# Score tiles of the first batch kept in eight slots of one large buffer, its late store cut in two, and the second batch's scores and the first values moved to later steps

## The chip, the cores and the metric

One NeuronCore of a Trainium2 chip runs one program. The metric is device time in microseconds (us), the median of several executions. The parts of the core that matter here: TensorE (PE in the profile), VectorE (DVE), ScalarE (ACT), GpSimd (POOL), and SyncE (SP), whose queue issues every DMA of this kernel. Each of them runs its own list of instructions in order and waits on semaphores for the others.

## What is computed

Attention with a mixing of the heads before and after the softmax, and then a gated expert without a nonlinearity, over 8 batches (B), 12 heads (H), 448 positions (S) and head width 64 (D):

```
scores = scale * q @ k^T                              # per batch and head, 448 x 448
scores = einsum('bhij,hg->bgij', scores, w_pre)       # heads mixed
attn   = softmax over j
attn   = einsum('bhij,hg->bgij', attn, w_post)        # heads mixed again
x      = attn @ v                                     # to (8*448) x 768
out    = ((x @ w1) * (x @ w2)) @ w3 @ w_out
```

The weights of the expert come as 64-bit floats and are turned into pairs of 32-bit parts on the chip.

## The kernel before, in words

**Scores through DRAM.** The mixing of heads needs all 12 heads of one row i on the partitions, while q @ k^T yields one head at a time. So `qk` (L166) makes the scores of one group (b, p, c): batch b, pair of heads p, and 128 rows of i (c = 0 to 2; a group with c = 3 takes the last 64 rows of two pairs). Four matmuls write two PSUM banks, 0 and 1 for the first group of a step and 6 and 7 for a second one; ACT copies the two banks to an SBUF tile `st` of 128 x 2 x 448 floats (L179, L180); and SP stores the tile in `raw_d[b]` in DRAM at the start of the next step (448 KB; a group with c = 3 takes two stores of 224 KB). `fetch` (L195) reads `raw_d` back as tiles `r` with (i, head) on the partitions, four steps ahead of their use; two `r` buffers stand ready.

**Steps.** The main loop (L889) runs over steps n of 10 rows of i, 45 steps per batch. A fetch, mix, exponential and second mix handle two steps at once, so work comes in pairs of steps: in an even step the maxima (`largest`, DVE L227) and `exp` (ACT L235); in an odd step `scale`, `post` (PE L260, into the two banks `pso`) and the next `mix` (PE L220). `put` (ACT L274) copies `pso` into a tile `mt`, which gathers 150 columns of i for attn @ v. `av` (PE L301) multiplies `mt` with the values and writes PSUM bank 0; its first run stands in step 19, its second in step 21.

**Weights beside it.** In the first 49 steps (up to `SWITCH`) the fold w3 @ w_out fills PE's free time (`folding`, PE L360, 384 matmuls); the function `shares` gives steps 18 and later a number of fold matmuls by how much else each step has, among it the score groups. Its operands are converted from words: SP loads `cs`, ACT and DVE convert (L110, L121 to L124, L129), POOL subtracts (L130), two pieces in a pair of steps.

**The buffers that the change touches.** The first six score groups (0, p, 0) are made ahead of the loop and lie together in one large tile `sz`, the first of the two buffers of the tag `mt` (L774): 5376 of its 7200 columns. Their first 48 rows are stored at once (FIRST, L31), the other 80 rows in one late store of 1680 KB (L805, issued by `held()` in L881). Each later `st` tile comes from a pool with two buffers: `qp` for odd pairs p of batch 0, `kp` for even ones and for all other batches (L178). The first `mt` tile takes the second `mt` buffer; the second one, `mt[0, 1]`, takes the buffer of `sz`, and its first copy comes at the end of step 17.

**What sets the order.** The dictionary `qks` (L809 to L819) says which groups stand at the end of which step: one group of batch 0 in each of steps 0 to 14, then batch 1 at steps int(11 + i * 28/21), i = 0 to 20, so steps 11, 12, 13, 15, 16, 17, 19 and on to 37; each c = 0 group has its keys and queries loaded six steps earlier (`load_kq`, 448 KB). The six loads of the first batch's values (`load_v`, 256 KB each) stand in steps 6 to 11 (L930). SP uses eight DMA semaphores in turn, so each DMA waits until the one eight places before it has landed.

Of the kernel before, what the change touches and what calls it, by code (L numbers as in the profile page):

```python
# [6 lines left out]
F32 = mybir.dt.float32  # L7
# [8 lines left out]
B, H, S, D = 8, 12, 448, 64  # L16
DM, FF = 768, 1024
HP = H // 2
IB = 10
GI = H * IB  # L20
NB = -(-S // IB)
QT, NJ = 128, 4
# [5 lines left out]
PP = 64  # L28
JB = S // PP
SETS = NB * B // 2  # L30
FIRST = 48  # L31
# [4 lines left out]
N_UP, NS = 20, 50  # L36
DEEP = 5
ONE = 2
# [12 lines left out]
class Kernel:  # L51
# [108 lines left out]
    def parts(self, b, p, c):  # L160
# [3 lines left out]
        return [(self.kqs[b, p], j * PP, S) for p, j in pairs]  # L164

    def qk(self, b, p, c, banks):  # L166


        nc = self.nc
# [5 lines left out]
        if b == c == 0:  # L175
            st = self.sz[:, 2 * p:2 * p + 2]
        else:
            st = (self.qp if b == 0 and p % 2 else self.kp).tile([128, 2, S], F32, tag="st", name=f"st{b}_{p}_{c}", bufs=2)  # L178
        nc.scalar.copy(st[:, 0], ps[0])  # L179
# [7 lines left out]
        n = QT if b or c else FIRST  # L187
# [553 lines left out]
    def run(self):  # L741
        nc, tc = self.nc, self.tc
# [31 lines left out]
        self.sz = self.mp.tile([QT, NJ, H, GB * IB], F32, tag="mt", name="sz")  # L774
        self.sz = self.sz.rearrange("p j g i -> p (j g i)")[:, :H * S].rearrange("p (h j) -> p h j", h=H)
        w = self.kp.tile([128, 2, S], F32, tag="st", name="wpre_s", bufs=2)[:, 0, :PP]
# [4 lines left out]
        for p in self.pso:  # L781
            for s in range(2):
                at = (2 * NJ - 2 + s) * HK
# [11 lines left out]
        held = []  # L795
# [7 lines left out]
        for f in held:  # L803
            f()
        held = lambda: nc.sync.dma_start(self.raw_d[0][FIRST:QT], self.sz[FIRST:])  # L805

# [5 lines left out]
        for b in range(1, B):  # L812
            first, per = (11, 28 / 21) if b == 1 else ((b - 1) * NB - 6, NB / 21)
            units = [(b, p, c) for g in range(0, HP, 2) for p, c in [*itertools.product((g, g + 1), range(3)), (g + 1, 3)]]
            for i, (b, p, c) in enumerate(units):
                n = int(first + i * per) | (b > 1)
                qks.setdefault(n, []).append((b, p, c))
                if c == 0:
                    loads.setdefault(max(n - 6, 0), []).append((b, p))  # L819
# [57 lines left out]
        for m in range(LF // 2):  # L877
            self.fetch(m)
        next(fold_pieces)
        next(fold_pieces)  # L880
        held()  # L881
        next(fold_pieces)
# [6 lines left out]
        for n in range(N + 6):  # L889
# [38 lines left out]
            if n + 3 < HP:  # L928
                others(n + 3)
            elif HP <= n < 2 * HP:  # L930
                self.load_v()
# [120 lines left out]
```

## Time and profile before

| | |
|---|---|
| median of 3 executions | 1441.89 us (1441.69 to 1447.07) |
| the profiled execution | 1437.83 us |
| its span, first to last instruction | 1436.1 us |
| mean granted TensorE clock | 0.986 |
| busy share of the span: PE, ACT, DVE, POOL | 96%, 58%, 52%, 43% |
| DMA over the span | 416.87 MB, mean 290 GB/s |

Times of single instructions are counted from the start of the span. A row of the timeline gives the start, the length and the instruction, and in brackets how long the engine had been idle before it and what ended that. A row of the waits gives the waiting engine and line, what it waited for, the sum in us, the number of times and the longest. A row of the windows gives each engine's busy time in a stretch, the granted clock (1.00 is full speed), the busy share of the DMA engines and what they moved.

### The profile page before, as it was taken

Reading aid. Unit: us, or ns where it says so; the run is one execution under the profiler, and the core shown is the slowest. Engines: PE = TensorE matmul, PEld = TensorE weight load, DVE = VectorE, ACT = ScalarE, POOL = GpSimd, SP = SyncE. Lnnn points to the kernel's source line nnn. Section 1 sums busy time; section 2 is a strip of 40 time slices with the busy share of each in tenths; the row PEclk is TensorE's granted clock in tenths of the full one; section 3 lists DMA queues with packets and bytes.
Section 4 is the critical chain, followed back from the end, with each engine's and each line's share of the span. In section 5 each row is a group of like instructions: output and inputs, shape, how many; then the busy total and the mean of one; then the engine's idle time right before and its main releaser. Section 6 shows DMA issues by size and latency. Waiting matters only on the chain.

```text
span 1436.1 us, 45775 instructions
## 1 busy us (share of the span) xinstructions
PE 1382.4 (96%) x18684; PEld 1055.2 (73%) x18684; DVE 741.1 (52%) x1497; ACT 832.4 (58%) x1952; POOL 620.3 (43%) x754
## 2 busy tenths in 40 slices
PE   5889999999999999999999999999999999999998
PEld 2457786776677667776777777777777777899988
DVE  6867566767544544432444436334444446345563
ACT  4867666777766666665656556556555445422231
POOL 2433233434433544532345336334335446446693
PEclk7989999999999999999999999999999999999999
DMA  8998789999999999999989979799879757698775
GB/s 294 366 326 279 236 270 322 320 312 317 324 286 348 355 356 330 362 346 349 287 275 290 320 259 280 249 323 354 288 229 281 241 177 223 195 337 270 231 232 171
DMA packets 203761, 416.87 MB, mean 290 GB/s; under 512 B 20528, under 2 KB 120112, under 8 KB 203472
## 3 DMA queue, kind: packets, MB, share of 16 engines
q1 hardware_dynamic: 203552, 413.94, 87.6%
q8 instruction: 149, 2.44, 0.7%
q14 instruction: 60, 0.49, 0.1%
HBM read 279.77 MB, written 134.09 MB: 288 GB/s over the span
## 4 chain that ended last, share of the span: by engine, by line
PE 82%; DMA 8%; DVE 4%; ACT 2%; issue 1%; POOL 1%; SPq 0%; DVEq 0%; POOLq 0%; ACTq 0%
PE e L702 21%; PE psa L301 11%; PE pso L260 10%; PE psm L220 9%; PE psq L174 7%; PE eg L522 5%; PE psf L360 4%; PE eo L553 4%; PE e2o L702 4%; PE e1o L702 4%; PE e3o L702 4%; DMA wu<-w_d 3%; DMA r<-raw_d 2%; DMA raw_d<-st 2%; ACT e L235 1%
## 5 line engine op out<-in xcount | busy, mean ns | idle before, releaser
L247 POOL TENSOR_SCALAR w<-wpo,ri 128x60 f32<-128x60 f32 x360 | 180.7, 518 | 485.1 <-DVE ri L245 465.3
L227 DVE TENSOR_REDUCE mn<-psm 128x1 f32<-128x448 f32 x360 | 207.7, 618 | 321.6 <-PE psm L220 321.3
L274 ACT COPY mt<-pso 128x480 f32<-128x480 f32 x352 | 197.9, 621 | 185.8 <-PE pso L260 185.6
L702 PE MATMUL e<-eh,wu 128*128 128x448 f32 x1008 | 296.8, 371 | 6.4 <-DVE c L656 3.2
L235 ACT ACTIVATE e<-psm,mn 128x448 f32<-128x448 f32 x360 | 226.8, 643 | 7.9 <-DVE mn L227 7.9
L702 PEld LDWEIGHTS e<-eh,wu 128*128 128x128 f32 x1008 | 187.5, 188 | 52.2 <-issue 26.8
L260 PEld LDWEIGHTS pso<-w,e 60*64 60x64 f32 x10080 | 175.2, 135 | 51.0 <-issue 42.5
L220 PE MATMUL psm<-r,wsc 60*64 60x448 f32 (+1 forms) x1440 | 191.2, 550 | 19.1 <-DVE cx L124 8.3
L260 PE MATMUL pso<-w,e 60*64 60x60 f32 x10080 | 199.1, 224 | 0.4 <-ACT mt L274 0.3
L702 PE MATMUL e<-el,wu 128*128 128x448 f32 x504 | 186.9, 371 | 0.0
L301 PE MATMUL psa<-mt,v 128*64 128x150 f32 (+1 forms) x2304 | 156.9, 292 | 4.1 <-ACT st L179 4.1
L301 PEld LDWEIGHTS psa<-mt,v 128*64 128x64 f32 x2304 | 143.6, 137 | 20.1 <-ACT st L179 6.7
L174 PE MATMUL psq<-kq 64*64 64x448 f32 x1176 | 154.6, 542 | 2.4 <-ACT st L179 2.4
L656 DVE TENSOR_TENSOR c<-c,e 128x448 f32<-128x448 f32 x168 | 101.7, 618 | 87.7 <-PE e L702 82.9
L179 ACT COPY st<-psq 128x448 f32<-128x448 f32 x162 | 86.4, 533 | 73.7 <-ACT mt L274 34.1
L522 PE MATMUL eg<-xh,wu 128*128 128x448 f32 x384 | 119.2, 381 | 6.3 <-DMA wu<-w_d 6.3
L641 POOL TENSOR_TENSOR el<-x,eh 128x448 fp32r<-128x448 f32 x90 | 103.7, 1170 | 32.8 <-ACT eh L640 29.9
L702 PEld LDWEIGHTS e<-el,wu 128*128 128x128 f32 x504 | 94.6, 188 | 22.5 <-issue 14.1
L174 PEld LDWEIGHTS psq<-kq 64*64 64x64 f32 x1176 | 60.8, 135 | 56.4 <-issue 28.8
L522 PEld LDWEIGHTS eg<-xh,wu 128*128 128x128 f32 x384 | 71.9, 190 | 38.7 <-issue 24.0
L244 DVE TENSOR_SCALAR sa<-sm 128x2 f32<-128x2 f32 x180 | 34.9, 194 | 113.6 <-ACT e L235 113.1
L180 ACT COPY st<-psq 128x448 f32<-128x448 f32 x162 | 87.6, 541 | 0.0
(99 smaller groups left out, 2010.1 us busy)
## 6 DMA issues: line engine op xcount, KB each, us to landing
r<-raw_d SPq DMA_DIRECT2D x344, 210.0 KB, 5.1
raw_d<-st SPq DMA_DIRECT2D x138, 448.0 KB, 6.1
wu<-w_d SPq DMA_DIRECT2D x104, 384.0 KB, 6.7
wu<-s_d SPq DMA_DIRECT2D x96, 384.0 KB, 4.8
wu<-w_d SPq DMA_DIRECT2D x51, 512.0 KB, 5.5
kq<-kq SPq DMA_DIRECT2D x42, 448.0 KB, 7.0
wu<-s_d SPq DMA_DIRECT2D x36, 512.0 KB, 4.9
x<-x_d SPq DMA_DIRECT2D x72, 224.0 KB, 5.7
```

Source lines behind the costliest of these rows:

```text
L174: nc.tensor.matmul(ps[s][z * PP:(z + 1) * PP], t[rows, q:q + PP], t[rows, k:k + S], start=True, stop=True)
L220: nc.tensor.matmul(ps[s][c * PP:(c + 1) * PP, :S], self.wsc[k], r[k, c], start=True, stop=True)
L227: self.nc.vector.tensor_reduce(mn[:, s:s + 1], self.psm[m][s][:, :S], axis=AX.X, op=ALU.min)
L235: nc.scalar.activation(e, p[:, :S], AF.Exp, bias=mn[:, s:s + 1], scale=-1.0, accum_out=sm[:, s:s + 1])
L247: nc.gpsimd.tensor_scalar_mul(w2[:, s], self.wpo, ri[:, s:s + 1])
L260: nc.tensor.matmul(self.pso[c][z * PP:(z + 1) * PP, at:at + HK], e[k, j * PP:(j + 1) * PP], w2s[k, s], start=True, stop=True)
L274: self.nc.scalar.copy(dst.rearrange("p j g (s i) -> p j s g i", s=2), src)
L301: nc.tensor.matmul(self.psa[rows, g % 3, :W], v[:, j, rows], mt[:, j, 2 * g + s, :W], start=(j == 0), stop=(j == NJ - 1))
L522: nc.tensor.matmul(p, u[:, k % (K1 // 2), x], xs[y][:, k], start=(k == 0 and t == 0), stop=(k == K1 - 1 and t == 2))
L641: nc.gpsimd.tensor_tensor(lo, x, hi.bitcast(F32), op=ALU.subtract)
L656: nc.vector.tensor_tensor(a[out], a[to[0]], p, op=ALU.add)
L702: nc.tensor.matmul(p, w[:, k, x], ops[m, k][y], start=(k == 0 and t == 0), stop=(k == nk - 1 and t == 2))
```

## The change

Four edits. (1) Score tiles made up to step 14 (RING) lie in eight slots of 896 columns of the `sz` buffer, taken in turn: the first two are the free columns behind the first scores, the next ones overwrite slots of the first scores. Later tiles all come from `kp`; `qp` has no `st` tiles any more. (2) The late store is cut into rows 48 to 63 (344 KB), issued ahead of the next load of words, and rows 64 to 127 (1376 KB), issued one place later. (3) Batch 1's groups stand at steps int(14 + 1.2 i): 14, 15, 16, 17, 18, 20 to 24, 26 to 30, 32 to 36 and 38; the loads of their keys move with them. (4) The loads of the first values stand in steps 11 to 16.

```diff
-DEEP = 5
+DEEP, RING = 5, 14
...
+    def next_st(self, name):
+        if self.step > RING:
+            return self.kp.tile([128, 2, S], F32, tag="st", name=name, bufs=2)
+        self.n_st += 1
+        at = (self.n_st + HP - 1) % 8 * 2 * S
+        return self.sz_all[:, at:at + 2 * S].rearrange("p (h j) -> p h j", h=2)
...
-            st = (self.qp if b == 0 and p % 2 else self.kp).tile([128, 2, S], F32, tag="st", name=f"st{b}_{p}_{c}", bufs=2)
+            st = self.next_st(f"st{b}_{p}_{c}")
...
-        self.sz = self.sz.rearrange("p j g i -> p (j g i)")[:, :H * S].rearrange("p (h j) -> p h j", h=H)
+        self.sz_all, self.n_st = self.sz.rearrange("p j g i -> p (j g i)"), 0
+        self.sz = self.sz_all[:, :H * S].rearrange("p (h j) -> p h j", h=H)
...
-        held = lambda: nc.sync.dma_start(self.raw_d[0][FIRST:QT], self.sz[FIRST:])
+        rest = [lambda k=k: nc.sync.dma_start(self.raw_d[0][k], self.sz[k]) for k in (slice(FIRST, PP), slice(PP, QT))]
...
-            first, per = (11, 28 / 21) if b == 1 else ((b - 1) * NB - 6, NB / 21)
+            first, per = (14, 1.2) if b == 1 else ((b - 1) * NB - 6, NB / 21)
...
+        rest[0]()
         next(fold_pieces)
         next(fold_pieces)
-        held()
+        rest[1]()
...
-            elif HP <= n < 2 * HP:
+            elif HP <= n - 5 < 2 * HP:
```

Where this moves instructions, first on SP's queue ahead of the loop. `r0` to `r2` are fetched score tiles, `cs3` to `cs5` words of weights, `kqz2` a piece of keys. Before:

```order
L202 DMA r1_222<-raw0_d_62 60x2x448 x2
L103 DMA cs3_225<-wo 128x768
L805 DMA raw0_d_62<-sz_136 80x5376
L103 DMA cs4_238<-wo 128x768
L103 DMA cs5_240<-wo 128x768
L873 DMA kqz2_128<-kq0 128x320
L202 DMA r2_258<-raw0_d_62 60x2x448 x2
L873 DMA kqz3_130<-kq0 128x320
```

And of the changed kernel, in the same place:

```order
L209 DMA r1_222<-raw0_d_62 60x2x448 x2
L813 DMA raw0_d_62<-sz_136 16x5376
L103 DMA cs3_226<-wo 128x768
L813 DMA raw0_d_62<-sz_136 64x5376
L103 DMA cs4_239<-wo 128x768
L103 DMA cs5_241<-wo 128x768
L881 DMA kqz2_128<-kq0 128x320
L209 DMA r2_259<-raw0_d_62 60x2x448 x2
L881 DMA kqz3_130<-kq0 128x320
```

The fetch `r2` needs rows 40 to 59, so of the late store it now waits for the first, smaller part alone; the second part still stands behind `cs3`.

The second place is ACT at the ends of steps 17 and 18 with the semaphores that each instruction waits for (DMAHW0 to DMAHW7 are those of SP's DMAs). `mt0_1` is the second `mt` tile, `st1_1_2` the tile of group (1, 1, 2). Before:

```order
L274 COPY mt0_0_414<-pso0_141 128x4x2x12x5 [waits PE_49]
L274 COPY mt0_1_1165<-pso1_142 128x4x2x12x5 [waits PE_49]
L179 COPY st1_1_2_1180<-psq1_1_2_0_1174 128x448 [waits DMAHW1_49,PE_49]
L180 COPY st1_1_2_1180<-psq1_1_2_1_1175 128x448 [waits PE_49]
L129 CAST fw1_1127<-cx20_1132 128x3x128 [waits DVE_49]
L110 ACTIVATE cm21_1196<-cs21_988 128x256 [waits DMAHW3_49,Activation_49]
L235 ACTIVATE e9_0_1214,sm9_1213<-psm9_0_1166,mn9_1191 128x448 [waits DVE_49]
```

And of the changed kernel:

```order
L281 COPY mt0_0_412<-pso0_141 128x4x2x12x5 [waits PE_49]
L281 COPY mt0_1_1130<-pso1_142 128x4x2x12x5 [waits DMAHW4_49,DMAHW3_49,DMAHW5_49,DMAHW2_49,DMAHW6_49,DMAHW1_49,DMAHW7_49,DMAHW0_49,PE_49]
L186 COPY st1_1_0_1145<-psq1_1_0_0_1139 128x448 [waits DMAHW6_49,PE_49]
L187 COPY st1_1_0_1145<-psq1_1_0_1_1140 128x448 [waits PE_49]
L129 CAST fw1_1092<-cx20_1097 128x3x128 [waits DVE_49]
L110 ACTIVATE cm21_1159<-cs21_939 128x256 [waits Activation_49]
L242 ACTIVATE e9_0_1176,sm9_1175<-psm9_0_1131,mn9_1154 128x448 [waits DVE_49]
L242 ACTIVATE e9_1_1178,sm9_1175<-psm9_1_1132,mn9_1154 128x448 [waits DVE_49]
L186 COPY st1_1_1_1194<-psq1_1_1_0_1188 128x448 [waits DMAHW2_49,PE_49]
```

The copy into `mt0_1` has got waits for DMAs, those of the stores out of the slots. Behind it two score tiles, of steps 17 and 18, each wait for a DMA: with `kp`'s two buffers these are the stores of the groups of steps 15 and 16, (1, 0, 1) and (1, 0, 2). Before, there was one such tile here, (1, 1, 2), which waits for the store of (1, 1, 0).

The third place is PE from the mix of step 17 to the first values matmuls in step 19. Before:

```order
L220 MATMUL psm9_1_1167<-r9_980,wsc_138 64x448
L174 MATMUL psq1_1_2_0_1174<-kq1_1_682 64x448
L174 MATMUL psq1_1_2_1_1175<-kq1_1_682 64x448
L174 MATMUL psq1_1_2_0_1174<-kq1_1_682 64x448
L174 MATMUL psq1_1_2_1_1175<-kq1_1_682 64x448
L360 MATMUL psf1_0_1203<-fo_148,fw0_227 128x384 x19
L301 MATMUL psa0_0_0_1235<-mt0_0_414,v0_0_540 64x150 x8
```

And of the changed kernel:

```order
L227 MATMUL psm9_1_1132<-r9_932,wsc_138 64x448
L181 MATMUL psq1_1_0_0_1139<-kq1_1_769 64x448
L181 MATMUL psq1_1_0_1_1140<-kq1_1_769 64x448
L181 MATMUL psq1_1_0_0_1139<-kq1_1_769 64x448
L181 MATMUL psq1_1_0_1_1140<-kq1_1_769 64x448
L367 MATMUL psf1_0_1166<-fo_148,fw0_228 128x384 x16
L181 MATMUL psq1_1_1_0_1188<-kq1_1_769 64x448
L181 MATMUL psq1_1_1_1_1189<-kq1_1_769 64x448
L181 MATMUL psq1_1_1_0_1188<-kq1_1_769 64x448
L181 MATMUL psq1_1_1_1_1189<-kq1_1_769 64x448
L308 MATMUL psa0_0_0_1205<-mt0_0_412,v0_0_767 64x150 x8
```

A score group now stands between step 18's folds and the first values matmul, and step 18 has 16 folds where it had 19. Counted from the start of the program, the groups of scores ahead of the first values matmul are 26 where they were 27, and the folds 40 where they were 43.

## The prediction

> **What bounds the kernel now.** I read the page first, then the windows, then who waited for whom in the first 100 us.
>
> ```profile
> span 1436.1 us, 45775 instructions
> PE 1382.4 (96%) x18684; PEld 1055.2 (73%) x18684; DVE 741.1 (52%) x1497; ACT 832.4 (58%) x1952; POOL 620.3 (43%) x754
> ```
>
> PE is busy for 96% of the span, so 54 us are idle. The windows show where the change works: busy us of each engine with its instructions, granted clock, DMA share, GB/s.
>
> ```profile
> core 0: us, PE busy (x) PEld busy (x) DVE busy (x) ACT busy (x) POOL busy (x), PEclk, DMA share, GB/s
> 31.00:58.00 27.00, 22.55 (x348) 11.11 (x348) 25.47 (x49) 23.96 (x58) 12.72 (x17) 0.94 1.02 360
> 58.00:72.00 14.00, 11.56 (x172) 6.13 (x166) 11.18 (x23) 9.26 (x23) 5.23 (x7) 0.87 1.03 374
> 72.00:85.00 13.00, 9.31 (x95) 4.75 (x88) 6.66 (x13) 9.28 (x22) 3.82 (x5) 0.50 1.04 377
> 85.00:96.00 11.00, 8.54 (x106) 5.39 (x99) 9.46 (x18) 6.49 (x16) 3.94 (x5) 0.99 1.01 351
> 111.00:220.00 109.00, 108.36 (x1504) 85.98 (x1500) 69.70 (x145) 71.98 (x174) 31.50 (x46) 1.00 0.84 266
> ```
>
> There are three stretches. Up to 58 us DVE is nearly full (25.47 of 27 us). From 58 to 96 us no engine is full, PE's clock sinks to half, and the DMA engines are busy throughout at 351 to 377 GB/s. From 111 us PE has hardly a gap (108.36 of 109), and DMA has room. After about 96 us, then, PE's work sets the end, and what counts is when PE gets there and how much work it has done by then.
>
> ACT's timeline shows the waits that the change aims at (start, length, instruction, idle before):
>
> ```profile
> 51.43 0.61 ACT L235 ACTIVATE e<-psm,mn 128x448 f32<-128x448 f32 x1
> 58.19 0.64 ACT L235 ACTIVATE e<-psm,mn 128x448 f32<-128x448 f32 x1
> 70.45 0.53 ACT L179 COPY st<-psq 128x448 f32<-128x448 f32 x1 [2.90 <-PE psm L220]
> 74.11 0.53 ACT L179 COPY st<-psq 128x448 f32<-128x448 f32 x1 [2.69 <-DMA raw_d<-st]
> 90.57 1.10 ACT L274 COPY mt<-pso 128x480 f32<-128x480 f32 x2
> 95.72 0.53 ACT L179 COPY st<-psq 128x448 f32<-128x448 f32 x1 [4.05 <-DMA raw_d<-st]
> 97.33 0.64 ACT L235 ACTIVATE e<-psm,mn 128x448 f32<-128x448 f32 x1
> ```
>
> The exponentials of steps 8 and 10 stand 6.76 us apart: that is the engines' own pace for a pair of steps. Step 18's comes at 97.33, although four such pairs would end at 58.19 + 4 * 6.76 = 85.2. The copies at 74.11 and 95.72 wait for a store to free their tile. The one at 70.45 names PE, but its matmuls were long done; its tile is that of step 9's group, whose store left late, so it is a DMA too. The last wait is the one that PE feels:
>
> ```profile
> 60.29 1.77 PE L220 MATMUL psm<-r,wsc 60*64 60x448 f32 x8
> 90.58 3.59 PE L360 MATMUL psf<-fo,fw 128*128 128x384 f32 x19
> 96.31 3.28 PE L301 MATMUL psa<-mt,v 128*64 128x150 f32 x48 [2.13 <-ACT st L179]
> 101.14 0.98 PE L174 MATMUL psq<-kq 64*64 64x448 f32 x8
> 106.47 3.28 PE L301 MATMUL psa<-mt,v 128*64 128x150 f32 x48 [0.64 <-ACT st L179]
> ```
>
> Step 19's first values matmul (96.31) writes bank 0, so it waits for the copy at 95.72, which waits for the store of group (1, 1, 0). I call this copy the gate.
>
> **Part by part: the slots.** They remove the waits for tiles in steps 11 to 14 (the 2.90 and 2.69 above, and shorter ones). But the gate moves, it does not go. The changed order has two tiles behind each other from `kp`, in steps 17 and 18; the second waits for the store of (1, 0, 2), and the values matmul waits for that copy. So I ask when that store lands. SP's queue:
>
> ```profile
> 31.59 1.21 SPq L202 DMA_DIRECT2D r<-raw_d  x2
> 87.56 0.35 SPq L188 DMA_DIRECT2D raw_d<-st  x1
> ```
>
> The first row is the fetch `r3` (step 2), in the same place in both kernels; the second is the store of (1, 1, 0), which landed when the gate opened, at 95.7. From one to the other, both counted, SP's program has 62 transfers before. Up to the new gate's store it has 62 in the changed kernel. I added them up with the sizes of this answer for 31 to 88 us (KB each, median us to landing):
>
> ```profile
> DMA packets 9389, 20.98 MB, mean 368 GB/s; under 512 B 979, under 2 KB 4334, under 8 KB 9381
> raw_d<-st SPq DMA_DIRECT2D x15, 448.0 KB, 7.5
> cs<-wo SPq DMA_DIRECT2D x11, 384.0 KB, 7.9
> r<-raw_d SPq DMA_DIRECT2D x16, 210.0 KB, 7.4
> v<-v SPq DMA_DIRECT2D x6, 256.0 KB, 7.2
> kq<-kq SPq DMA_DIRECT2D x3, 448.0 KB, 7.3
> ```
>
> Before: 15 score stores of 448 KB, 16 fetches of 210, six values loads, three keys loads, the words and some smaller ones, 20.58 MB. Changed: one score store less, one load of words more, the rest equal, 20.51 MB. DMA moved 20.98 MB in these 57 us and was never idle. So the same bytes stand ahead of the gate, and it opens at the same time, though ACT and PE come to it earlier: step 17's mix, which needs `r9`, could run at 60.29 + 3 * 6.76 = 80.6.
>
> What can shift it: if DMA ran at the 377 GB/s of the best window all the way, 56 us would shrink by 1.3. On the other side, values and one keys load worth 1.5 MB (4 * 256 + 448 KB) leave the time before step 10, where DVE sets the pace; if that left DMA hungry for the 0.4 MB by which 344 GB/s falls short of the measured 360 (344 is what the changed order asks for: 9.16 MB by its count from `r3` to step 10's fetch, at 31.6 and 58.2 us), the gate would come 1.2 later. The late store adds up to 1.3 earlier (below). So between -2.6 and +1.2 us; I take -0.5, as a small part of the slack before 31 us should come through.
>
> **The late store.** The fetch `r2` now waits for 344 KB only:
>
> ```profile
> SPq L202 <- DMA raw_d<-sz: 5.5, 3, 4.5
> DVE cx L121 <- DMA cs<-wo: 2.6, 1, 2.6
> DMA  3999958997989999999999999999999999988696
> ```
>
> (The last row is DMA's busy share in tenths, in 40 slices from 0 to 110 us.) The 4.5 us are SP's wait in front of `r2`; it should go, and other transfers fill DMA, which I bound at 1.3 us: the two slices of 2.75 us after 24.75 with a 7 and an 8 leave 0.8 and 0.5 us unused. It does not quicken the engines by itself: DVE's 2.6 us there are a wait for words (`cs4`) that stand behind the same bytes as before, and from then on DVE is full.
>
> **The new wait for the `mt` buffer.** The second copy of the pair at 90.57 must now wait until the slots' last stores have landed, those of step 14's groups. They stand nine transfers ahead of the new gate's store, so they land some 8 us before it, at about 87. Queued behind it on ACT are step 17's score tile (which waits for a store four places ahead of the gate, to about 91) and step 18's exponential. None of it is later than the gate: nothing, as long as the gate is where I put it; up to 1 us if ACT's work behind the wait piles up.
>
> **The moved scores.** PE's total work is the same, but less of it lies ahead of 96 us, where PE waits anyway: one group less (0.98 us, the row at 101.14) and three folds less (3 * 3.59 / 19 = 0.57). These 1.55 us now lie where PE is full. Moreover step 34 gets a group that step 33 had, right ahead of step 35's values matmul; such a neighbour costs 0.64 (the row at 106.47): +0.65, or nothing if the copy is early. The moved values loads are needed from step 19; issued up to step 16 they are inside the 62, so they cost nothing more.
>
> **The clock.** With the engines early and the gate not, PE has a longer hole. After step 18's 16 folds (at about 86) the next scores need banks 0 and 1, which step 17's copies free at about 92; one group of 1 to 2 us, then a second hole up to the gate. Before, PE worked from 85 to 94 and met the gate at full clock. What a hole does (PE busy, clock, DMA share, GB/s):
>
> ```profile
> 12.00:15.00 3.00, 0.00 (x0) 0.77 0.85 262
> 15.00:18.00 3.00, 0.00 (x0) 0.50 0.72 186
> 27.00:30.00 3.00, 2.47 (x14) 0.50 1.03 325
> 30.00:33.00 3.00, 3.00 (x15) 0.50 0.91 270
> 33.00:36.00 3.00, 3.00 (x73) 0.82 1.04 383
> ```
>
> Six idle us brought the clock to 0.50, and it came back about 5.5 us after steady work began at 28. At half clock that would cost 5.5 / 2 = 2.75 us behind the gate; nothing, if the clock stays. The group at 92 may start the return early, so I take half, 1.4.
>
> The Trainium skill, TensorE: Matmul & The Clock Gate, section on what is actually happening, says that the gate knows only half and full clock, and that one busy window of about 3.4 us brings back full clock; an estimate from that page is 1.7 us for this term. The clocks of 0.50 and 1.00 in these rows agree (0.77 and 0.82 are windows with both); this trace's return took longer. By the page's figure with no help from the group at 92 the sum below would be 0.3 us higher.
>
> **The sum.** -0.5 + 1.55 + 0.65 + 1.4 = +3.1 us on the profiled execution's own time, 1437.83: 1440.9. The median of the runs shown lies 4.06 higher, at 1441.89, and I shift it by the same: 1445.0. The bounds give -2.6 + 1.55 = -1.1 and +1.2 + 1 + 1.55 + 0.65 + 2.75 = +7.2, so 1440.8 to 1449.1.
>
> **The rivals.**
>
> Faster: the bytes do not set the gate, but the tiles did. Then the engines keep their pace: step 17's mix at 80.6, then 1.8 for it, 1 for a group, 3 for 16 folds, 1 for a group and 0.5 for its copy put the first values matmul at 87.9, 8.4 earlier. With 1.55 and 0.65 back, -6.2: 1435.7. For it: the waits at 70.45 to 95.72 name tiles. Against: the DMA share of 1.0 over 38 us, and two `kp` tiles behind each other.
>
> Slower: two `kp` buffers are too few for runs of five. From step 20 on groups now stand in runs of five neighbouring steps instead of three, so in each of three runs three tiles instead of one must find the store of two steps earlier landed. The landing times after 97 us:
>
> ```profile
> DMA to landing us min/median/max: 2.9/4.2/5.0
> ```
>
> and two neighbouring mixes, one pair of steps apart:
>
> ```profile
> 125.50 0.97 PE L220 MATMUL psm<-r,wsc 60*64 60x448 f32 x7
> 132.74 0.97 PE L220 MATMUL psm<-r,wsc 60*64 60x448 f32 x7
> ```
>
> Two steps last 7.24 us, a store 4.2 and at most 5.0 plus up to 1 until SP issues it. It decides from a landing of over some 6 us. If landings were those of the crowded stretch (about 8.1 us), each of nine tiles would wait some 0.9: 8.1 more, 1453.1. Against it: DMA has room there (266 GB/s).
>
> That the slots are not what they say, with each copy waiting for the store just before it, is ruled out by the waits in the order: each names one DMA, that of its own slot.
>
> **How the numbers follow.** Forecast 0.75, faster rival 0.15, slower rival 0.10. The range reaches past the forecast's bounds toward the faster rival, the likelier of the two: 1438.0 to 1449.5. Half a per cent, 7.2 us, is about what a measurement of this kernel can tell from no change. The faster rival, at -6.2, would mostly stay inside it: faster 0.05. The slower one lies outside for the larger part: slower 0.08. Same 0.87.
>
> **What would show it.** Right: the copy of step 18's group waits for `raw_d`, the first values matmul starts at 94 to 97 us, PE has a hole of several us between 85 and 95, the clock there falls to 0.5 and the copy into `mt` waits for a DMA to 86 to 88. Wrong: the first values matmul before 92 (the bytes did not bind), or waits for `raw_d` on ACT after 105 us (two buffers too few), or a wait for words on DVE before 58 us (the late store's first part cost something).

## The result, and the profile after

| | before | after |
|---|---|---|
| median | 1441.79 us (6 executions, 1440.97 to 1447.07) | 1451.63 us (6 executions, 1448.34 to 1458.74) |
| the profiled execution | 1437.83 us | 1458.74 us |
| its span | 1436.1 us | 1456.9 us |
| mean granted clock | 0.986 | 0.978 |

The ratio is 1.0073, with a 95% interval of 1.0052 to 1.0094: 10.5 us more (7.5 to 13.6; the two medians alone differ by 9.8), where 3.1 us were forecast. The direction was the forecast's, the size was three times as large.

The two profiled executions are no fair pair as wholes: before's lies 4 us under the median of its kernel, after's 7 us over its own. Much of that difference arises late in the span, as the part on the wrong prediction shows. So I read the traces up to about 211 us of before, where the score groups of batch 1 and the fold work of the forecast have their effect, and use the timed ratios for the whole.

PE's row of the page of after:

```profile
PE 1394.0 (96%) x18684; PEld 1060.6 (73%) x18684; DVE 740.2 (51%) x1497; ACT 832.6 (57%) x1952; POOL 618.3 (42%) x754
```

PE is busy 11.6 us longer for the same 18684 matmuls, and all of that lies behind step 47, at 210.85 us of before and 218.52 of after: from there to the end PE is busy 11.7 us longer. Up to there it is busy equally long in both. What after loses up to there is idle time, since work that is moved to a later place leaves a hole where it stood. The windows of after, with the same columns as before:

```profile
58.00:72.00 14.00, 10.20 (x164) 5.44 (x160) 13.20 (x27) 12.46 (x31) 6.76 (x9) 0.88 1.01 362
72.00:85.00 13.00, 9.21 (x165) 5.30 (x168) 12.27 (x24) 12.01 (x31) 5.83 (x9) 1.00 1.01 334
85.00:96.00 11.00, 5.76 (x31) 3.33 (x24) 5.03 (x9) 3.86 (x10) 2.71 (x3) 0.82 0.99 334
```

From 58 to 85 us the slots do what they should: DVE and ACT are nearly full (12.27 and 12.01 of 13 us in the second window, 6.66 and 9.28 before), so the waits for tiles there are gone. Then the engines stop: between 85 and 96 us PE is busy for 5.76 of 11 us, against 8.54 before. ACT's timeline shows on what:

```profile
74.51 0.62 ACT L242 ACTIVATE e<-psm,mn 128x448 f32<-128x448 f32 x1
81.26 0.63 ACT L242 ACTIVATE e<-psm,mn 128x448 f32<-128x448 f32 x1
89.12 0.61 ACT L281 COPY mt<-pso 128x480 f32<-128x480 f32 x1 [3.54 <-DMA raw_d<-sz]
93.33 0.53 ACT L186 COPY st<-psq 128x448 f32<-128x448 f32 x1 [3.59 <-DMA raw_d<-st]
97.83 0.53 ACT L186 COPY st<-psq 128x448 f32<-128x448 f32 x1 [1.56 <-DMA raw_d<-st]
```

The exponentials of steps 14 and 16 stand 6.75 us apart: the pace of the engines. Behind them three waits for DMA follow each other: the copy into the `mt` buffer that waits for the slots' last stores, step 17's score tile, and step 18's, which is the gate. PE in the same stretch:

```profile
85.61 3.07 PE L367 MATMUL psf<-fo,fw 128*128 128x384 f32 x16
93.92 2.20 PE L181 MATMUL psq<-kq 64*64 64x448 f32 x8 [5.24 <-ACT st L186]
98.42 5.14 PE L308 MATMUL psa<-mt,v 128*64 128x150 f32 x48 [2.30 <-ACT st L186]
```

The first values matmul starts at 98.42 (96.31 before), after holes of 5.24 and 2.30 us, and its 48 matmuls take 5.14 us instead of 3.28: PE has lost its clock. The windows around it:

```profile
89.00:92.00 3.00, 0.00 (x0) 0.00 (x0) 0.31 (x1) 0.61 (x1) 0.00 (x0) 1.00 1.00 335
92.00:95.00 3.00, 1.08 (x5) 0.58 (x8) 0.00 (x0) 1.67 (x5) 0.21 (x1) 0.50 0.95 299
95.00:98.00 3.00, 1.12 (x7) 0.00 (x0) 1.33 (x3) 1.44 (x6) 1.62 (x3) 0.50 1.07 366
98.00:101.00 3.00, 2.58 (x22) 2.46 (x24) 0.00 (x0) 0.80 (x2) 0.00 (x0) 0.50 1.05 378
101.00:104.00 3.00, 3.00 (x64) 2.73 (x61) 0.00 (x0) 0.40 (x1) 0.00 (x0) 0.79 0.26 103
```

The rest of the loss lies where PE is full. Step 19's mix, the first behind that run, starts 3.96 us later than before, and step 47's, the mix at which both kernels have made the same groups and the same folds in all, 7.67 us later. The four rows, of before:

```profile
100.38 0.54 PE L220 MATMUL psm<-r,wsc 60*64 60x448 f32 x1
210.85 0.54 PE L220 MATMUL psm<-r,wsc 60*64 60x448 f32 x1
```

and of after:

```profile
104.34 0.54 PE L227 MATMUL psm<-r,wsc 60*64 60x448 f32 x1
218.52 0.54 PE L227 MATMUL psm<-r,wsc 60*64 60x448 f32 x1
```

From the one mix to the other it is 110.47 us before and 114.18 after, 3.71 more, where the forecast has 1.55 + 0.65 = 2.2. PE's groups by line between these two mixes, of before (lines 360, 174 and 301 are folds, scores and values; busy us and mean ns, then idle us):

```profile
L360 PE MATMUL psf<-fo,fw 128*128 128x384 f32 x322 | 60.6, 341 | 0.0
L174 PE MATMUL psq<-kq 64*64 64x448 f32 x152 | 18.6, 542 | 0.0
L301 PE MATMUL psa<-mt,v 128*64 128x150 f32 x144 | 9.8, 293 | 1.3 <-ACT st L179 1.3
```

and of after:

```profile
L367 PE MATMUL psf<-fo,fw 128*128 128x384 f32 x325 | 62.3, 342 | 0.0
L181 PE MATMUL psq<-kq 64*64 64x448 f32 x160 | 19.6, 548 | 0.0
L308 PE MATMUL psa<-mt,v 128*64 128x150 f32 x144 | 9.8, 293 | 1.9 <-ACT st L186 1.9
```

One group more costs 1.0, as forecast, and the extra wait 0.6, as forecast. But three folds more cost 1.7 instead of 0.57. Where that comes from is seen in PE's timeline, 26 folds in one run before:

```profile
112.21 4.81 PE L360 MATMUL psf<-fo,fw 128*128 128x384 f32 x26
119.47 2.88 PE L360 MATMUL psf<-fo,fw 128*128 128x384 f32 x15
```

and 26 folds of after with a group in between:

```profile
123.47 3.05 PE L367 MATMUL psf<-fo,fw 128*128 128x384 f32 x16
126.45 0.98 PE L181 MATMUL psq<-kq 64*64 64x448 f32 x8
127.37 2.03 PE L367 MATMUL psf<-fo,fw 128*128 128x384 f32 x10
```

The two parts last 3.05 + 2.03 = 5.08 us, the whole 4.81. From runs of 15 and 26 a fold costs (4.81 - 2.88) / 11 = 0.175 us, and a run 2.88 - 15 * 0.175 = 0.25 besides. The folds between the two mixes stand in 17 runs before and in 21 after: four more of 0.25 to 0.3 (the latter by an experiment below) are the 1.1 that were missed. The fifth more of the groups in even steps, that of step 34, stands at the end of its run and cuts none. In the forecast every fold cost 3.59 / 19 = 0.19, with the run's own cost hidden in that mean.

These busy times overlap at their ends. If each stretch is counted from its own start to the start of the next one, PE's timelines between the two mixes give 1.45 us more for the folds, 0.98 for the groups, 0.68 for the values with their waits, and 0.65 for the mixes, 3.76 in all. So a cut costs 0.23 us of time (three folds are 0.52 of the 1.45), and the mixes, whose work is the same, cost something too: in after four of them have no group behind them, and the folds start 0.91 us after such a mix (130.19 to 131.10), where a group starts 0.75 us after one (113.93 to 114.68).

Each trace thus gives three terms: when the first values run starts, how long it lasts over 3.28, and the time from the one mix to the other over 110.47. For after: 2.11 + 1.86 + 3.71 = 7.68, the 7.67 that step 47's mix is late. This lies inside the interval of the timed difference, at its lower end.

### The profile page after: what moved, and what is told of

It reads as the page before. It is cut to its first block, busy times and chain, and to the rows that moved or that the text cites. A ratio compares the mean times of both kernels' runs of the same rounds, so it can differ in the third digit from the quotient of the medians.

```text
span 1456.9 us, 45762 instructions
## 1 busy us (share of the span) xinstructions
PE 1394.0 (96%) x18684; PEld 1060.6 (73%) x18684; DVE 740.2 (51%) x1497; ACT 832.6 (57%) x1952; POOL 618.3 (42%) x754
## 3 DMA queue, kind: packets, MB, share of 16 engines
q8 instruction: 149, 2.44, 0.7%
## 4 chain that ended last, share of the span: by engine, by line
PE 83%; DMA 8%; DVE 4%; ACT 2%; issue 1%; SPq 1%; POOL 1%; DVEq 0%; POOLq 0%; ACTq 0%
PE e L709 20%; PE psa L308 11%; PE pso L267 11%; PE psm L227 9%; PE psq L181 7%; PE eg L529 6%; PE psf L367 4%; PE eo L560 4%; PE e2o L709 4%; PE e3o L709 4%; PE e1o L709 3%; DMA wu<-w_d 2%; DMA r<-raw_d 2%; DMA raw_d<-st 1%; DMA raw_d<-sz 1%; DVE mn L234 1%
## 5 line engine op out<-in xcount | busy, mean ns | idle before, releaser
L227 PE MATMUL psm<-r,wsc 60*64 60x448 f32 (+1 forms) x1440 | 195.6, 557 | 21.9 <-DMA r<-raw_d 14.9
L181 PE MATMUL psq<-kq 64*64 64x448 f32 x1176 | 157.7, 547 | 6.8 <-ACT st L186 6.8
L186 ACT COPY st<-psq 128x448 f32<-128x448 f32 x146 | 78.0, 534 | 76.9 <-ACT mt L281 33.9
L315 ACT COPY xd<-psa 128x450 f32<-128x450 f32 (+1 forms) x36 | 19.2, 533 | 118.5 <-PE psa L308 118.5
```

Source lines behind the costliest of these rows:

```text
L181: nc.tensor.matmul(ps[s][z * PP:(z + 1) * PP], t[rows, q:q + PP], t[rows, k:k + S], start=True, stop=True)
L227: nc.tensor.matmul(ps[s][c * PP:(c + 1) * PP, :S], self.wsc[k], r[k, c], start=True, stop=True)
```

## The experiments

Each kernel was timed against the kernel before on the same chip, in three sessions (median of before 1445.82 in the first, 1443.68 in the second, 1443.70 in the third). The first values run in each of the eleven traces, which the table behind them takes apart. In the order of the table, after the row of after:

Late store alone:

```profile
97.54 3.28 PE L301 MATMUL psa<-mt,v 128*64 128x150 f32 x48 [1.53 <-ACT st L179]
```

After with the late store whole:

```profile
97.31 4.60 PE L308 MATMUL psa<-mt,v 128*64 128x150 f32 x48 [1.76 <-ACT st L186]
```

Moved scores and values alone:

```profile
97.07 6.22 PE L301 MATMUL psa<-mt,v 128*64 128x150 f32 x48 [2.45 <-ACT st L179]
```

Slots alone:

```profile
95.88 6.04 PE L308 MATMUL psa<-mt,v 128*64 128x150 f32 x48 [4.15 <-ACT st L186]
```

Moved scores alone:

```profile
97.69 3.28 PE L301 MATMUL psa<-mt,v 128*64 128x150 f32 x48 [2.80 <-ACT st L179]
```

Moved values loads alone:

```profile
97.11 4.95 PE L301 MATMUL psa<-mt,v 128*64 128x150 f32 x48 [3.12 <-ACT st L179]
```

After with step 18's group in step 19:

```profile
94.95 4.96 PE L308 MATMUL psa<-mt,v 128*64 128x150 f32 x48 [3.09 <-ACT st L186]
```

After with four tiles:

```profile
92.58 4.95 PE L309 MATMUL psa<-mt,v 128*64 128x150 f32 x48 [1.43 <-ACT st L187]
```

Slots and four tiles, old steps, late store whole:

```profile
91.96 3.28 PE L309 MATMUL psa<-mt,v 128*64 128x150 f32 x48 [1.17 <-ACT st L187]
```

The same with slots up to step 12 only:

```profile
94.53 3.28 PE L310 MATMUL psa<-mt,v 128*64 128x150 f32 x48
```

After with fewer groups in even steps:

```profile
99.34 5.55 PE L308 MATMUL psa<-mt,v 128*64 128x150 f32 x48 [0.81 <-ACT st L186]
```

The terms in us, each against before (96.31, 3.28 and 110.47); the sum is how much later step 47's mix starts; the last column is the timed ratio with its interval:

| kernel | start | length | between the mixes | sum | timed |
|---|---|---|---|---|---|
| after | +2.11 | +1.86 | +3.71 | +7.67 | 1.0073 (1.0052 to 1.0094) |
| late store alone | +1.23 | 0 | -0.03 | +1.20 | 1.0008 (0.9994 to 1.0021) |
| after, late store whole | +1.00 | +1.32 | +3.65 | +5.97 | 1.0060 (1.0046 to 1.0074) |
| moved scores and values | +0.76 | +2.94 | +3.68 | +7.38 | 1.0050 (1.0031 to 1.0069) |
| slots alone | -0.43 | +2.76 | +0.08 | +2.41 | 1.0002 (0.9986 to 1.0018) |
| moved scores alone | +1.38 | 0 | +3.98 | +5.36 | 1.0064 (1.0051 to 1.0077) |
| moved values loads alone | +0.80 | +1.67 | +0.01 | +2.48 | 1.0015 (1.0000 to 1.0031) |
| after, step 18's group in 19 | -1.36 | +1.68 | +3.94 | +4.25 | 1.0034 (1.0019 to 1.0048) |
| after with four tiles | -3.73 | +1.67 | +3.68 | +1.63 | 1.0013 (0.9996 to 1.0031) |
| slots, four tiles | -4.35 | 0 | +0.13 | -4.22 | 0.9971 (0.9954 to 0.9989) |
| slots to step 12, four tiles | -1.78 | 0 | -0.04 | -1.82 | 0.9978 (0.9960 to 0.9996) |
| after, fewer even groups | +3.03 | +2.27 | +2.53 | +7.83 | one execution, 1449.94 us |

The sums say from single traces what the ratios say from many executions: the largest difference is that of the moved scores alone, 5.36 against 9.2 us. The third column is the steadiest. It is within 0.15 of 0 in the five kernels with the old steps, and 3.65 to 3.98 in the six with the new ones as they are or with one group moved. Each kernel has one trace only, so what the first two owe to the single execution is not shown; the last part shows that the clock can go either way behind the same hole.

**The late store alone.** Before, with this:

```diff
-        held = lambda: nc.sync.dma_start(self.raw_d[0][FIRST:QT], self.sz[FIRST:])
+        rest = [lambda k=k: nc.sync.dma_start(self.raw_d[0][k], self.sz[k]) for k in (slice(FIRST, PP), slice(PP, QT))]
...
+        rest[0]()
         next(fold_pieces)
         next(fold_pieces)
-        held()
+        rest[1]()
```

> The kernel before with the late store in two parts and nothing else. Theory A (the first part, ahead of the words cs3, makes every later transfer issue later and the engines never make it up): the words cs4 land at about 30.5 us instead of 28.1, step 3's mix stands at 37.0 instead of 34.3, the first values matmul 1.5 to 2.5 us later than the 96.3 of before, the total 1.5 to 3 us longer. Theory B (the delay at the start is absorbed, since the same bytes are due at the gate; the moved scores make the whole difference): step 3's mix may be late, but the first values matmul stands within 0.7 us of before and the total within 1 us.

Measured: 1445.25 us, no difference that can be told; the first values run starts 1.23 later, between the two forecasts. By step 3's mix the trace is 3.25 us behind before's, and most of that is made up again by step 19. So the two parts show no gain; the interval of the ratio leaves room for a cost of up to 3 us.

**After, with the late store whole.** This edit undoes the one above in the changed kernel.

```diff
-        rest = [lambda k=k: nc.sync.dma_start(self.raw_d[0][k], self.sz[k]) for k in (slice(FIRST, PP), slice(PP, QT))]
+        held = lambda: nc.sync.dma_start(self.raw_d[0][FIRST:QT], self.sz[FIRST:])
...
-        rest[0]()
         next(fold_pieces)
         next(fold_pieces)
-        rest[1]()
+        held()
```

> The changed kernel with the late store in one part again (slots and moved scores kept). A: step 3's mix at 34.3, the first values matmul at 95.5 to 96.5 at half clock, the total 6 to 7.5 us above before, 2 to 3 less than the changed kernel. B: the first values matmul as in the changed kernel, 98 to 98.5, and the total 9 to 10 above before.

Measured: 1453.74 us, still 0.60% slower. That is 8.7 us, between the two forecasts. The late store is not where most of the loss is. The gate opens 1.1 us earlier than in after, the counterpart of the 1.23 above.

**The moved steps alone.** Before, with the new steps of the scores and of the values:

```diff
-            first, per = (11, 28 / 21) if b == 1 else ((b - 1) * NB - 6, NB / 21)
+            first, per = (14, 1.2) if b == 1 else ((b - 1) * NB - 6, NB / 21)
...
-            elif HP <= n < 2 * HP:
+            elif HP <= n - 5 < 2 * HP:
                 self.load_v()
```

> The kernel before with only the second batch's scores from step 14 and the values loads five steps later; tiles from the two pools and one late store as before. A: the waits for tiles hold PE back ahead of the gate, so the hole in front of it is smaller and the clock stays up; the first values matmul at 95.5 to 96.5, the total 2 to 5 us above before (1.55 of work moved behind the gate, 0.65 for one more neighbour, and up to 2 for clock). B (the moved scores are the whole of it): 9 to 10 above. If the slots are what costs, within 1 us of before plus the 2.2 of moved work.

Measured: 1452.51 us, 0.50% slower. Most of the loss is in this part of the change.

**The slots alone.** Before, with the tiles of the change:

```diff
-DEEP = 5
+DEEP, RING = 5, 14
...
-            st = (self.qp if b == 0 and p % 2 else self.kp).tile([128, 2, S], F32, tag="st", name=f"st{b}_{p}_{c}", bufs=2)
+            st = self.next_st(f"st{b}_{p}_{c}")
```

> The kernel before with only the eight slots; late store in one part, scores and values loads in the steps of before. A: ACT's waits for tiles in steps 11 to 14 are gone, the gate stays the third tile from the two-buffer pool (step 17's), so the first values matmul stands at 95 to 96.5 and the total within 1 us of before; a hole of several us in front of the gate and a clock of 0.5 there would add up to 2. If tiles were the bound and not the bytes: first values matmul at 88 to 92 and the total 4 to 8 below before.

Measured: 1445.86 us, ratio 1.0002: nothing. Step 15's mix starts 4.41 us earlier than before's, and the first values run only 0.43: the time won from 58 to 85 us is lost again in front of the gate, and the hole of 4.15 us there costs PE its clock besides.

**The moved scores alone, and the moved values loads alone.** The two halves of the diff of the moved steps, each in the kernel before. First the scores:

```diff
-            first, per = (11, 28 / 21) if b == 1 else ((b - 1) * NB - 6, NB / 21)
+            first, per = (14, 1.2) if b == 1 else ((b - 1) * NB - 6, NB / 21)
```

> The kernel before with only the second batch's scores from step 14 on; values loads in steps 6 to 11 as before. If the moved scores are what costs: from the mix of step 19 to that of step 47 3.7 us more than before, the first values matmul at 96 to 97.5, mostly at half clock, the total 5 to 8 us above before, as with both moves. If the values loads, crowded into steps 11 to 16, are what costs: within 2.5 us of before.

Measured: 1452.36 us, 0.64% slower: as much as the whole change loses, within the intervals, and more than the 5 to 8 us expected. The time between the mixes came as expected, the half clock did not: in this trace the values run at full clock. Then the loads:

```diff
-            elif HP <= n < 2 * HP:
+            elif HP <= n - 5 < 2 * HP:
                 self.load_v()
```

> The kernel before with only the first values loaded five steps later. If the bytes ahead of the gate are what counts, the order of these loads among them changes nothing: first values matmul within 1 us of 96.3 and the total within 1.5 us of before. If the loads, crowded into steps 11 to 16, are what costs: the gate comes 1.5 to 3 us later and the total is 2 to 5 us above before.

Measured: 1444.93 us, ratio 1.0015 with an interval that just touches 1. Most of the loss is that of the moved scores.

**After, with step 18's group in step 19.** If two `kp` tiles behind each other right ahead of the first values hold the gate, one of them moved behind it must open it.

```diff
                 n = int(first + i * per) | (b > 1)
+                if b == 1 and n == 18:
+                    n = 19
```

> The changed kernel with one group of scores, that of step 18, put in step 19 instead (behind the first values matmuls). If the first values matmul waits for the store that stands last ahead of it (my gate): it now waits for step 17's copy only, whose store stands four transfers earlier; in the changed kernel that copy came at 93.3, so the first values matmul stands at 93 to 95 instead of 98.4, and with one group less ahead of it the total is 2 to 4 us below the changed kernel, 6 to 8 above before. If the gate is not what holds PE there: first values matmul at 97 or later and the total as in the changed kernel.

Measured: 1449.71 us, 0.34% slower. The first values run starts at 94.95 instead of 98.42. ACT now waits for step 17's tile only:

```profile
94.36 0.53 ACT L186 COPY st<-psq 128x448 f32<-128x448 f32 x1 [3.87 <-DMA raw_d<-st]
```

So the gate was where the forecast put it. Moving it back wins 3.5 us there, and between the mixes nothing: 3.94, against 3.71 in after.

**Four tiles.** From step 15 on every other tile of batch 1 comes from the fold's pool, so that a tile as a rule waits for the store of four groups earlier. First in the kernel after:

```diff
-    def next_st(self, name):
+    def next_st(self, name, b, p, c):
         if self.step > RING:
-            return self.kp.tile([128, 2, S], F32, tag="st", name=name, bufs=2)
+            pool = self.fp if b == 1 and (p + c) % 2 else self.kp
+            return pool.tile([128, 2, S], F32, tag="st", name=name, bufs=2)
```

> The changed kernel with four tiles instead of two for the second batch's scores after step 14 (every other one from the fold's pool). If two tiles and the stores behind them make the gate: ACT's waits of 3.6 and 1.6 for raw_d in steps 17 and 18 go, only the wait of the copy into mt (to about 89) stays; first values matmul at 91 to 93, at half or full clock, the total 5 to 7 us below the changed kernel, 3 to 5 above before. If the bytes hold everything whatever the tiles (the next fetch or the words would be late instead): first values matmul at 96 or later, total within 2 of the changed kernel.

Measured: 1444.94 us, ratio 1.0013, against 1.0073 without the four tiles; the two intervals do not meet. The first values run comes at 92.58, 5.8 us earlier than in after. Then the same with the old steps and the whole late store, that is before with slots and four tiles (`RING` and `sz_all` as in the change):

```diff
+    def next_st(self, name, b, p, c):
+        if self.step > RING:
+            pool = self.fp if b == 1 and (p + c) % 2 else self.kp
+            return pool.tile([128, 2, S], F32, tag="st", name=name, bufs=2)
+        self.n_st += 1
+        at = (self.n_st + HP - 1) % 8 * 2 * S
+        return self.sz_all[:, at:at + 2 * S].rearrange("p (h j) -> p h j", h=2)
```

> The eight slots and the four tiles together, the late store in one part and scores and values loads in the steps of before. If tiles are what holds: the only wait left is that of the copy into mt for the slots' last stores, to about 90; first values matmul at 91 to 93 and the total 2 to 5 us below before. If the bytes hold: first values matmul at 95 to 97 and the total within 1 us of before.

Measured: 1440.37 us, ratio 0.9971 (0.9954 to 0.9989): faster than both kernels, by 0.3%. The first values run starts 4.35 earlier, at full clock. What is late next is the copy into the `mt` buffer, on ACT:

```profile
90.88 0.61 ACT L282 COPY mt<-pso 128x480 f32<-128x480 f32 x1 [5.04 <-DMA cs<-w3t]
```

The row names a load of words, which the copy does not need; it overwrites the buffer in which the slots lie, and so waits for their last stores. To take that wait away as well, the next kernel ends the slots at step 12 and takes all later tiles up to step 39 from the four in turn:

```diff
-DEEP, RING = 5, 14
+DEEP, RING = 5, 12
...
-            pool = self.fp if b == 1 and (p + c) % 2 else self.kp
+            self.n_late = getattr(self, "n_late", 0) + 1
+            pool = self.fp if self.n_late % 2 and self.step < 40 else self.kp
```

> The slots up to step 12 only, and four tiles taken in turn from step 13 on; one late store, scores and values loads in the steps of before. If the copy into mt, which waits to 90.9 for the slots' last stores, is what is left of the gate: that wait goes, the first values matmul stands at 88 to 91 instead of 92.0, and the total is 1 to 4 us below the kernel with slots to step 14 and four tiles, 5 to 8 below before. If the next thing due is the bytes of the fetches (step 17's mix) or a tile again: first values matmul at 91.5 to 93 and the total within 1 us of that kernel.

Measured: 1440.26 us, ratio 0.9978: the same as with slots up to step 14, within the intervals. The first values were expected at 88 to 91. PE has no hole in front of them, yet they come at 94.53, since the waits stand earlier and PE loses its clock there: 19 folds take 5.26 us instead of 3.59. ACT:

```profile
86.63 0.53 ACT L188 COPY st<-psq 128x448 f32<-128x448 f32 x1 [4.10 <-DMA raw_d<-st]
```

and PE:

```profile
84.97 1.77 PE L229 MATMUL psm<-r,wsc 60*64 60x448 f32 x8 [2.98 <-DMA r<-raw_d]
89.34 5.26 PE L369 MATMUL psf<-fo,fw 128*128 128x384 f32 x19
```

Without the slots in steps 13 and 14 a tile waits again, 4.10 us, and PE waits for a fetch. Which of the two decides was not tried. The wait in front of the copy into `mt` is gone, and nothing is won by it.

**After, with fewer groups in even steps.** From step 20 on the changed kernel has ten groups in even steps, before has five; an even step's folds are cut by a group, while in an odd step it stands between the mix and the folds. This list leaves seven in even steps from step 20 on, and as many groups in all:

```diff
                 n = int(first + i * per) | (b > 1)
+                if b == 1:
+                    n = (14, 15, 16, 17, 18, 20, 21, 23, 24, 25, 26, 27, 29, 30, 31, 32, 33, 34, 35, 37, 38)[i]
```

> The changed kernel with the same 21 groups from step 14 to 38, but from step 20 on seven of them in even steps where the changed kernel has ten (an even step's group cuts a run of fold matmuls in two). In the traces so far a run of n fold matmuls lasts about 0.31 + 0.172 n us. If the cut runs are the part of the price that I missed: from the mix of step 19 to that of step 47, 3.7 us more than before in all three kernels with the moved scores, it falls by 3 * 0.31 = 0.9, to about 2.8. If not: 3.5 to 3.9 as there.

Measured: one execution, 1449.94 us. The folds between the two mixes stand in 18 runs instead of 21, and the group of their rows reads:

```profile
L367 PE MATMUL psf<-fo,fw 128*128 128x384 f32 x325 | 61.4, 341 | 0.0
```

61.4 against 62.3 in after: 0.9 for three runs, 0.3 each. Between the mixes it is 2.53 instead of 3.71, so 1.18 less. Counted from start to start, the folds take 0.70 less and the mixes 0.41, three of which have got their group back. The cost of a cut, and that of a mix without a group behind it, are thus shown in both directions.

## Why the prediction was wrong

**What bounds the kernel: right.** Up to the first values PE waits for DMA, behind them it is full, and both terms passed on to the end: the order of the kernels by the sums is close to that by the timed ratios.

**The moved scores: the mechanism was right, the term too small.** This step failed in every kernel that has it: "These 1.55 us now lie where PE is full" and "+0.65" make 2.2; measured were 3.71 in after, and 3.65 to 3.98 in the other kernels that keep all the new steps. The group (1.0) and the neighbour (0.6) have their forecast sizes. The step "three folds less (3 * 3.59 / 19 = 0.57)" priced folds by their mean in a run of 19, and did not see that five more groups in even steps cut runs of folds: three folds and four more runs cost 1.7 in busy time and 1.45 from start to start. Nor has it a term for the four mixes that lost the group behind them, 0.65. With these nothing of the 3.71 is left over.

**"The gate moves, it does not go": right.** The copy of step 18's group waits for `raw_d`, the copy into `mt` waited to 89.1 (86 to 88 forecast), and the kernels that move a tile behind the gate, or use four, open it.

**"It opens at the same time": wrong, "I take -0.5", measured +2.11.** In the trace of after this is the largest miss, 2.6 us against 1.5 for the moved scores, and it lies outside the bounds of -2.6 to +1.2. The count of bytes held: from the fetch `r3` to the gate's store DMA moved about as much as was counted. DMA in after from 33 to 91 us:

```profile
DMA packets 9595, 20.52 MB, mean 354 GB/s; under 512 B 978, under 2 KB 4951, under 8 KB 9586
```

But two things that the count takes as given were not the same: `r3` started later, and the rate was 354 GB/s instead of 368. SP's queue of after:

```profile
17.86 2.47 SPq L813 DMA_DIRECT2D raw_d<-sz  x1
20.37 2.88 SPq L103 DMA_DIRECT2D cs<-wo  x2
23.29 2.49 SPq L881 DMA_DIRECT2D kqz<-kq  x1
25.89 1.87 SPq L209 DMA_DIRECT2D r<-raw_d  x2
33.16 0.80 SPq L209 DMA_DIRECT2D r<-raw_d  x2
90.50 0.51 SPq L195 DMA_DIRECT2D raw_d<-st  x1
```

`r3` starts at 33.16 instead of 31.59 (+1.57), the gate's store at 90.50 instead of 87.56 (+2.94, so 1.37 more on the way, where the rate was lower), and it lands in 7.3 us instead of 8.1 (-0.8): together +2.1. The late start of `r3` comes from the cut store: with the late store alone `r3` starts at 33.72, and in after with the late store whole at 31.64.

**The late store: the wait went, the gain did not come.** "The 4.5 us are SP's wait in front of `r2`; it should go": it went, as the rows above show, where `r2` follows the keys' issue at once. But `r2` starts only 1.1 us earlier than before, at 25.89 instead of 26.99, because the issues ahead of it take longer. In before the late store's issue took 0.42 us:

```profile
17.18 0.42 SPq L805 DMA_DIRECT2D raw_d<-sz  x1
```

In after that of the second part takes 2.47, the two of words behind it 2.88 (2.82 before) and that of keys 2.49 (1.96 before). So the words `cs4` were issued at 20.37 instead of 17.65, and the longest wait for words on DVE grew, from 2.6 us to 4.9 (3.0 in after with the late store whole), which the prediction names as the sign that this part cost something. From the waits of after, 20 to 58 us:

```profile
DVE cx L121 <- DMA cs<-wo: 5.8, 2, 4.9
```

The cover "a wait for words that stand behind the same bytes as before" was counted in bytes and not in issues. The "up to 1.3 earlier" became 1.1 to 1.2 later at the gate, by the two pairs of traces that differ in this alone. Why the issues take longer was not tried. (The 344 and 1376 KB of the two parts are thousands of bytes; in the unit of the other sizes they are 336 and 1344, of 1680.)

**The clock: right in kind, 1.86 against 1.4.** That the middle of 0 and 2.75 came so near is luck: over the twelve changed kernels' traces this term goes from 0 to 2.94. The 5.5 us that it rests on is also read a little short: in windows of 1 us the clock of before is back at 34.0, which is 6.0 after 28.

**The rivals.** The slower one, two buffers too few for runs of five, did not happen: after 105 us ACT waits for no `raw_d` at all up to 230 us. The price it gave, 1453.1, is near the result for another reason. The faster one stated a choice that does not exist here, bytes or tiles: the tiles say whose store the gate waits for, the queue says when that store lands. With four tiles in the changed kernel the gate came 5.8 us earlier through the same queue.

**Behind step 47.** From that mix to the end after takes 13.1 us longer than before, for the same work: 11.7 us are PE's busy time and 1.4 idle time. The busy time is the clock. Behind step 47 before has one stretch at half clock, 3.4 us long; after has six, 27.3 us in all, and half of the 23.9 more is 12. The last part shows one of them. They lie where both kernels run the same matmuls, so this trace does not show them to be a cost of the change; before's profiled execution met only one. In the other kernels PE is busy behind step 47 for 2.5 to 6.4 us more than in before's trace.

**What stays open.** The sum of after is 7.67, the timed difference 10.5 (7.5 to 13.6). The moved scores alone have 5.36 against 9.2 (7.4 to 11.1). The trace of the moved scores alone has no clock term, where that of the moved scores and values has 2.94; whether most executions have one was not tried.

## What to carry to other kernels

Before work is moved from a stretch where the bottleneck engine waits to one where it is full, price it there with its start costs: count how many runs of the long, uniform work it cuts, not only how much work it is. A wait for a buffer that is taken away in one place is only worth something if the next wait in line is taken away too; here eight slots alone gave nothing, and eight slots with four later tiles gave 0.3%. When kernels are compared by one trace each, compare PE's busy time for the same work as well, since a few stretches at half clock can exceed the effect that is looked for. Where the argument is that the same bytes lie ahead, check that the transfers' issue keeps its pace as well.

## What the runs showed of the hardware

**A hole of the same length costs PE its clock in one run and not in another.** Behind step 47 both kernels run the same matmuls. The same mix, in before and then in after:

```profile
302.51 1.22 PE L220 MATMUL psm<-r,wsc 60*64 60x448 f32 x5 [1.36 <-ACT e L235]
310.67 2.38 PE L227 MATMUL psm<-r,wsc 60*64 60x448 f32 x8 [1.35 <-ACT e L242]
```

The holes in front of it are 1.36 and 1.35 us long, and those before them 0.26 and 0.27. In before the clock stays at 1.00 (windows from 300 to 308), in after it is 0.61 from 310 to 312 and 0.53 from 312 to 314. The other way round, one load of weights later on leaves a hole of 2.44 us in before (to 1100.05) at a clock of 1.00, and in after one of 1.91 us (to 1119.41) that costs the clock.

**The half clock comes in multiples of one length.** Followed in windows of 0.5 us, the stretches at half clock are 3.41 us long (after from about 310, 502, 1018 and 1119; before from about 522), 6.83 (after from about 532 and 686), 10.24 (after from about 92, ahead of the first values and in them) or 13.65 (before from about 72), each a multiple of 3.41. With PE busy throughout, one costs half of that, 1.7 us: three of the kernels in the table have a clock term of 1.67 or 1.68.

The Trainium skill, TensorE: Matmul & The Clock Gate, Part 1 on the clock gate, says that the gate judges PE's activity in windows of about 3.4 us that run freely, whatever the program does. These traces agree with that: the lengths are multiples of 3.41 us, and equal holes fare differently. A single price for the clock in a forecast, as the 1.4 here, is therefore only the middle of a range.

**Busy DMA engines are not always equally fast.** At a busy share of 1.01 DMA moved 362 GB/s from 58 to 72 us of after and 334 from 72 to 85. The share alone told nothing of the 4% by which the way to the gate was slower. Why the rate fell was not tried.
